# Layer 2's w_in decoded one stage sooner, its w_out sooner too, one output group of eight, and longer transfers in the plan for the first tiles

## The chip, the cores and the metric

The kernel runs on one core of one Trainium2 chip. The metric is the device time of one execution in microseconds (us), the median of several runs.

## The reference

What is computed is an attention in chunks, whose result goes through two layers of the same shape with different gates (cut to what matters):

```python
# attention, for each chunk of 32 queries (4 batches, 8 heads, 768 positions, 64 wide)
k_full = np.concatenate([mem_k, k[c0 - 16:c0 + 40]], axis=2)   # 8 memory rows, then the window
v_full = np.concatenate([mem_v, v[c0 - 16:c0 + 40]], axis=2)
out[c0:c0 + 32] = softmax(q_c @ k_full.T / sqrt(64)) @ v_full

x = out.transpose(0, 2, 1, 3).reshape(3072, 512)
# layer 1: w_in 512 x 2048, w_out 2048 x 512
h = x @ w_in;  x = (h * clip(h + 3, 0, 6) / 6) @ w_out
# layer 2: other weights
h = x @ w_in;  g = h if h >= 1, 0 if h <= -1, else ((h + 1) / 2) ** 2
out = g @ w_out
```

## The kernel before

Everything is fp32 on the outside; each product of two fp32 matrices is made of three matmuls on operands that are split into a high and a low part ("hi" and "lo"). The weights arrive as 64-bit words ("wpk"). A weight tile of 128x512 is turned into hi and lo on the chip, by `decoded` and what calls it: a load into `raw` (L318), a shift on ACT (L325) or on DVE (L327), a rebase on ACT (L331), a join on DVE (L335), a cast to hi on ACT (L303) and a subtraction for lo on DVE (L366).

Tokens come in six tiles of 512. Tiles 0 and 1 go through layer 1 directly, right behind their attention: `hidden` (matmuls L866 to L868, gate L875 on ACT and L878 on DVE, split into ghi L886 on ACT and glo L887 on DVE) and `project` (L902 to L904). Attention of a block is: scores (PE L748, from `q_sb` and the windows `kx` that POOL copies at L625 and L626), exponent (ACT L772), norm (DVE L778 to L782), a flip of the weights by TensorE (L789) whose result `tp` is copied to `tr` (L303, on ACT or DVE), the values (PE L800 into `pv`), and the split into xhi (ACT L847) and xlo (DVE L848). Before the first hidden matmuls stand nine matmuls on the identity (L1440) that only keep TensorE busy.

All later tiles go in pairs, by a scheme that needs seven products where the plain one needs eight. Layer 1 has the stages (0,1) and (0,2), layer 2 the stages (1,0), (1,1) and (1,2). A stage has eight steps of `hidden_pair` (PE L1027 to L1029; ACT copies a bank at L1010, DVE adds the other at L1014; gate: ACT L1074, DVE L1082) and output products. In stage (0,1) the output is `project`; in the others it is `out_pair` (PE L1264 to L1266), over groups of hidden steps. A group sums its products in PSUM, and where a stage has more than one group, the partial results are added up in `csum` (DVE L1242 and L1236, ACT L1234). `SEVEN` lists the groups of each stage: (0,2) has two groups of four, (1,0) and (1,1) one group of eight.

Layer 2's weights are decoded while layer 1 runs. `weight_pair` takes two w_in tiles: the decoding, four subtractions of 128x256 on DVE (L457), casts on ACT (L468, L471, L472) and subtractions on DVE (L469, L473, L476); its results go out to memory (`wfs`) and come back when they are used. For w_out it is `weight` and `combine_out` (subtractions L496, cast L509, subtraction L510, stores to `wcs`).

What sets the order of the work is a planner that is part of the kernel: every operation is added with an engine and a cost, a key (a due time in the planner's own units) and a list of tasks that must be done before; the planner runs a list schedule with a limited number of buffers (pools "w", "s", "in", "lv" and others), and the order that comes out is the order of the instructions on each engine. For a transfer the size that the planner reckons with is `kb`. It does not change the transfer itself.

The lines of the change: L617 in `load_block` (queries and keys of one block), L676 in `load_values` (values of one block), L1090 (`SEVEN`), L1406 (keys of `weight_pair`) and L1409 (keys of layer 2's w_out tiles).

Of the kernel before, what the change touches and what calls it, by code (L numbers as in the profile page):

```python
# [38 lines left out]
NK = 2 * NF  # L39
# [222 lines left out]
def fused_kernel(ctx: ExitStack, tc: tile.TileContext, qkv, qk, vv, wpk, const, out):  # L262
    nc = tc.nc
# [28 lines left out]
    add = plan.add  # L292
# [305 lines left out]
    def load_block(j, key):  # L598

        early = key < 0

        over = key > NF
        far = 3 * (not early)
        w = KB + KC if wide(j) else KB
        q = q_buf[j] = Buf(
            ["in"] + ["w"] * ((early or over) and not wide(j)), [128, NP * (QB + w)], F32, "q_sb",
            **({"w": 1} if early else {}),
        )  # L610
        if j < NEARLY:
            src = qkv[j, :, :WQ]
        else:
            src = qk[2 * (j - NEARLY):2 * (j - NEARLY) + 2].rearrange("g d w -> (g d) w")
        after = [*last_w, *later.get(j * NCH // NSB // 4, ())] if over else ()
        if not wide(j):
            add(("SP", 430), key - 6 - far * (key > 4) - 2.5 * early, lambda e: nc.sync.dma_start(tile_of(q), src), writes=[(q, 0)], kb=448, after=after, line="load")  # L617
            kx = kx_buf[j] = Buf(["w", "st"], [128, NP, 2, KC], F32, "kx", w=2, st=1)

            def windows(e):  # L620
                k = tile_of(q)[:, NP * QB:].rearrange("p (a t) -> p a t", a=NP)
                at = k[:, :, NMEM + CHUNK:KC + CHUNK]
                p, a, t = at.ap
                X = {"DVE": V, "POOL": G}[e]
                X.tensor_copy(tile_of(kx)[:, :, :, NMEM:], type(at)(at.tensor, at.offset, [p, a, (CHUNK, 2), t]))  # L625
                X.tensor_copy(tile_of(kx)[:, :, :, :NMEM], k[:, :, :NMEM].unsqueeze(2).to_broadcast([128, NP, 2, NMEM]))  # L626

            kx.made = add(("DVE", 700) if j < 2 else ("POOL", 1300), key - 5 - 3.5 * early, windows, [(q, 0)], [(kx, 0)])
            return
        k4 = lambda: tile_of(q)[:, NP * QB:].rearrange("p (a t) -> p a t", a=NP)  # L630
        add(
            ("SP", 430), key - 6 - far, lambda e: nc.sync.dma_start(
                k4()[:, :, :KB], src[:, NP * QB:].rearrange("p (a t) -> p a t", a=NP)
            ), writes=[(q, 1)], kb=256, after=after, line="load",
        )
        add(
            ("SP", 430), key - 6 - far, lambda e: nc.sync.dma_start(tile_of(q)[:, :NP * QB], src[:, :NP * QB]),
            writes=[(q, 0)], kb=192, after=after, line="load",
        )

        def spread(e):
            k = k4()
            cast(e, k[:, :, KB + NMEM:], k[:, :, NMEM + CHUNK:KC + CHUNK])
            cast(
                e, k[:, :, 2 * CHUNK:2 * CHUNK + 2 * KC].rearrange("p a (b t) -> p a b t", b=2)[:, :, :, :NMEM],
                k[:, :, :NMEM].unsqueeze(2).to_broadcast([128, NP, 2, NMEM]),
            )

        add([("DVE", 425), ("ACT", 560)], key - 4.5, spread, [], [(q, 1)])

    def load_values(s, key):


        early = key < 0
        late = s * SB >= 2 * T
# [4 lines left out]
        n = 0  # L660

        def load(x, c, m, row, rows, step, j):

            nonlocal n
            if j < NEARLY:
                src = qkv[j, row:row + rows, WQ + W * x:WQ + W * (x + 1)]
            else:
                src = vv[2 * (j - NEARLY) + x, row:row + rows, :]
            lines, rest = src.ap
            src = type(src)(src.tensor, src.offset, [lines, (lines[0] * step, m), rest])  # L670
            p = 64 * x + row % CHUNK
            queue = "ACT" if s == 0 and x else "SP"
            add(
                (queue, 400), min(key - 2, -7.2) if early else key - 8,
                lambda e: (nc.scalar if e == "ACT" else nc.sync).dma_start(tile_of(v)[p:p + rows, c:c + m], src),
                writes=[(v, n)], kb=1.7 * rows * m if early else rows * m, line="load v" + queue,  # L676
                after=[kx_buf[s].made] if queue == "ACT" else later.get(s // 4, ()),
            )
            n += 1
# [3 lines left out]
        while c < NSB:  # L683
            j, i = divmod(s * NSB + c, NCH)
# [8 lines left out]
        if not late:  # L693
# [3 lines left out]
            while c < NSB:  # L697
                m = 1
# [365 lines left out]
    def gate(l, p, t, f, key, h, psum=False):  # L1064
# [22 lines left out]

    raw_g = {}
    SEVEN = {
        (0, 2): ((0, 1, 2, 3), (4, 5, 6, 7)), (1, 0): (tuple(range(8)),), (1, 1): (tuple(range(8)),), (1, 2): (tuple(range(6)), (6, 7)),  # L1090
    }
    BASE = (0, 29.25, 57.25, 85.25, 113.25)
    GMOST = 20
# [270 lines left out]
    for n, (l, p) in enumerate(pairs):  # L1364
# [38 lines left out]
            pair_x(*pairs[n + 1], base + 25, [done[n, 7 if seven else 5]], ["w"] if seven else ["in", "lv", "w"])  # L1403
        if n == 0:
            for i in range(NF // 2):
                weight_pair(i, base + 22 + 4 * i, [done[0, 5]])  # L1406
        if n == 1:
            for i in range(NF // 2):
                raws = [weight(1, 2 * i + x, 1, base + 20 + step * (i + 0.5 * x) - 3, [done[1, 3]]) for x in range(2)]  # L1409
                combine_out(i, raws, base + 20 + step * (i + 0.5) + 1)  # L1410

    with tc.manual_schedule():
# [98 lines left out]
```

## Time and profile before

| | |
|---|---|
| time, median of 3 runs | 1062.2 us (1061.84, 1062.2, 1065.2) |
| the profiled execution | 1067.35 us |
| its span in the profile | 1065.3 us |
| TensorE (PE) busy in the span | 1036.6 us, 97% |
| VectorE (DVE) busy | 835.9 us, 78% |
| ScalarE (ACT) busy | 679.8 us, 64% |
| DMA | 289.18 MB, mean 271 GB/s |

The profile is that of one execution. Busy time of TensorE is that of its matmuls, which overlap: each 128x512 matmul is shown with some 0.39 us, while the next one starts about 0.23 us behind it. So a busy share says less than the count of matmuls in a stretch and the idle times that the timeline shows in square brackets, with what ended them. PEclk is the granted clock as a share of full speed.

### The profile page before, as it was taken

To read this page: it belongs to the slowest core of one execution; us is meant where nothing else is said; L and a number is where in the kernel's file an instruction comes from. 1 tells how busy PE (TensorE), PEld (TensorE's weight loads), DVE (VectorE), ACT (ScalarE), POOL (GpSimd) and SP (SyncE) were. 2 spreads that over 40 slices of the span, in tenths; PEclk is the share of its full clock that TensorE was granted. 3 is DMA by queue.
4 is the path that set the end of the run, shared out by engine and by line. 5 is a ranking of instruction groups with operands and counts; after the bars stand their busy time and mean duration, and the time that the engine had idled before them with its cause. 6 is when DMAs were issued, how large, how long until landed. Compare 5 with 4: busy or idle time off the path is not lost.

```text
span 1065.3 us, 19872 instructions
## 1 busy us (share of the span) xinstructions
PE 1036.6 (97%) x7381; PEld 842.6 (79%) x7381; DVE 835.9 (78%) x1439; ACT 679.8 (64%) x1427; POOL 27.2 (3%) x49
## 2 busy tenths in 40 slices
PE   6899999999999999999999999999999999999998
PEld 5677787788878887878778788888888888888886
DVE  4897489856876689789899997799765899658654
ACT  5897457634655586666785698655577655676461
POOL 4220000000000000000000000000000000000000
PEclk9999999999999999999999999999999999999999
DMA  8999878873988689999899799855774755965603
GB/s 244 345 358 359 332 237 273 285 243 112 321 282 258 198 300 368 417 399 390 309 404 399 282 344 391 311 178 188 228 266 151 282 169 177 334 223 198 191 34 79
DMA packets 153760, 289.18 MB, mean 271 GB/s; under 512 B 12352, under 2 KB 97984, under 8 KB 153664
## 3 DMA queue, kind: packets, MB, share of 16 engines
q1 hardware_dynamic: 153232, 287.62, 76.9%
q8 instruction: 58, 0.95, 0.4%
q10 hardware_dynamic: 432, 0.30, 0.1%
q14 instruction: 38, 0.31, 0.1%
HBM read 206.08 MB, written 81.79 MB: 270 GB/s over the span
## 4 chain that ended last, share of the span: by engine, by line
PE 67%; DVE 16%; DMA 11%; ACT 3%; issue 2%; SPq 1%; POOL 0%; DVEq 0%; POOLq 0%; ACTq 0%
PE ph L1027 10%; PE ph L1028 9%; PE ph L1029 9%; PE po L1265 7%; PE po L1266 7%; PE po L1264 7%; DMA raw<-wpk 5%; DVE glo L887 4%; PE py L902 3%; PE py L904 3%; PE py L903 3%; DVE raw L335 2%; PE ph L866 2%; DVE g L1224 2%; PE ph L868 2%
## 5 line engine op out<-in xcount | busy, mean ns | idle before, releaser
L886 ACT CAST ghi<-g 128x512 fp32r<-128x512 f32 x234 | 145.0, 621 | 119.1 <-PE po L1266 78.8
L887 DVE TENSOR_TENSOR glo<-g,ghi 128x512 fp32r<-128x512 f32 x234 | 158.7, 686 | 37.5 <-ACT ghi L886 37.2
L1027 PE MATMUL ph<-xop,wf 128*128 128x512 f32 x448 | 175.2, 391 | 3.2 <-DVE s L1014 1.9
L1028 PE MATMUL ph<-xop,wf 128*128 128x512 f32 x448 | 174.5, 390 | 0.8 <-DVE xop L977 0.8
L1029 PE MATMUL ph<-xop,wf 128*128 128x512 f32 x448 | 174.4, 389 | 0.0
L1265 PE MATMUL po<-glo,ws 128*128 128x512 f32 x420 | 163.6, 390 | 0.4 <-DVE glo L887 0.4
L1266 PE MATMUL po<-ghi,ws 128*128 128x512 f32 x420 | 163.4, 389 | 0.0
L1264 PE MATMUL po<-ghi,ws 128*128 128x512 f32 x420 | 163.4, 389 | 0.0
L1074 ACT ACTIVATE r<-s,bias 128x512 f32<-128x512 f32 x120 | 86.6, 724 | 58.7 <-DVE s L1014 57.8
L1014 DVE TENSOR_TENSOR s<-s,ph 128x512 f32<-128x512 f32 x120 | 81.8, 685 | 43.4 <-PE ph L1029 36.5
L1027 PEld LDWEIGHTS ph<-xop,wf 128*128 128x128 f32 x448 | 84.1, 188 | 24.1 <-DVE s L1014 4.2
L902 PE MATMUL py<-ghi,w 128*128 128x512 f32 x256 | 102.5, 401 | 0.0
L1010 ACT COPY s<-ph 128x512 f32<-128x512 f32 x120 | 70.6, 588 | 47.7 <-PE ph L1029 43.8
L903 PE MATMUL py<-glo,w 128*128 128x512 f32 x256 | 100.2, 391 | 0.2 <-DVE glo L887 0.2
L904 PE MATMUL py<-ghi,w 128*128 128x512 f32 x256 | 99.9, 390 | 0.0
L1028 PEld LDWEIGHTS ph<-xop,wf 128*128 128x128 f32 x448 | 84.1, 188 | 18.0 <-DVE xop L977 1.2
L1029 PEld LDWEIGHTS ph<-xop,wf 128*128 128x128 f32 x448 | 84.1, 188 | 17.6
L1265 PEld LDWEIGHTS po<-glo,ws 128*128 128x128 f32 x420 | 78.8, 188 | 17.6 <-DVE glo L887 1.2
L1264 PEld LDWEIGHTS po<-ghi,ws 128*128 128x128 f32 x420 | 78.8, 188 | 16.5
L1266 PEld LDWEIGHTS po<-ghi,ws 128*128 128x128 f32 x420 | 78.9, 188 | 16.1
L1082 DVE SCALAR_TENSOR_TENSOR g<-r,s 128x512 f32<-128x512 f32 x104 | 71.5, 690 | 24.3 <-ACT r L1078 10.1
L1224 DVE TENSOR_TENSOR g<-g 128x512 f32<-128x512 f32 x120 | 81.1, 687 | 1.4
(132 smaller groups left out, 1775.1 us busy)
## 6 DMA issues: line engine op xcount, KB each, us to landing
raw<-wpk SPq DMA_DIRECT2D x64, 512.0 KB
ws<-wcs SPq DMA_DIRECT2D x60, 512.0 KB
wf<-wfs SPq DMA_DIRECT2D x48, 512.0 KB
ws<-wos SPq DMA_DIRECT2D x90, 256.0 KB
wf<-wfs SPq DMA_DIRECT2D x48, 384.0 KB
wos<-w SPq DMA_DIRECT2D x32, 512.0 KB
wcs<-wc SPq DMA_DIRECT2D x32, 512.0 KB
w<-wos SPq DMA_DIRECT2D x32, 512.0 KB
```

The lines of the kernel that those rows point to most:

```text
L886: add(("ACT", act(T)), key, lambda e: A.copy(tile_of(ghi), g()), [of], [(ghi, 0)], line="split")
L887: add(("DVE", dve(T)), key + 0.1, lambda e: V.tensor_tensor(out=tile_of(glo), in0=g(), in1=tile_of(ghi), op=ALU.subtract,), [of, (ghi, 0)] ...
L902: P.matmul(y, w2hi, gh, start=first, stop=False)
L903: P.matmul(y, w2hi, gl, start=False, stop=False)
L904: P.matmul(y, w2lo, gh, start=False, stop=last)
L1027: P.matmul(q, whi()[:, m], xh, start=first, stop=False, skip_group_check=True)
L1028: P.matmul(q, whi()[:, m], xl, start=False, stop=False, skip_group_check=True)
L1029: P.matmul(q, wlo()[:, m], xh, start=False, stop=c == 1, skip_group_check=True)
L1224: ("DVE", dve(T)), key, lambda e: V.tensor_tensor(out=o(), in0=i0(), in1=i1(), op=op),
L1264: P.matmul(q, wt[:, 0, m], xh, start=begin, stop=False, skip_group_check=True)
L1265: P.matmul(q, wt[:, 0, m], xl, start=False, stop=False, skip_group_check=True)
L1266: P.matmul(q, wt[:, 1, m], xh, start=False, stop=end, skip_group_check=True)
```

## The change

Four things change. The planner reckons with longer transfers: the first blocks' queries and keys count 605 instead of 448, and the values of all blocks of tiles 0 and 1 count 1.95 per row instead of 1.7 (for the first) or 1 (for the others). Stage (0,2) gets one output group of eight steps instead of two of four. Layer 2's w_in pairs get keys from the start of stage (0,1) on, six units apart, and may begin when that stage's first hidden step is done, instead of keys from 22 units into the stage, four apart, and behind its sixth step. Layer 2's w_out tiles get keys 6 units sooner, 3.2 units apart, and may begin behind the second hidden step of stage (0,2) instead of the fourth; the keys of `combine_out` stay.

```diff
-            add(("SP", 430), key - 6 - far * (key > 4) - 2.5 * early, lambda e: nc.sync.dma_start(tile_of(q), src), writes=[(q, 0)], kb=448, after=after, line="load")
+            add(("SP", 430), key - 6 - far * (key > 4) - 2.5 * early, lambda e: nc.sync.dma_start(tile_of(q), src), writes=[(q, 0)], kb=605 if early else 448, after=after, line="load")
...
-                writes=[(v, n)], kb=1.7 * rows * m if early else rows * m, line="load v" + queue,
+                writes=[(v, n)], kb=(1.95 - 0.95 * late) * rows * m, line="load v" + queue,
...
-        (0, 2): ((0, 1, 2, 3), (4, 5, 6, 7)), (1, 0): (tuple(range(8)),), (1, 1): (tuple(range(8)),), (1, 2): (tuple(range(6)), (6, 7)),
+        (0, 2): (tuple(range(8)),), (1, 0): (tuple(range(8)),), (1, 1): (tuple(range(8)),), (1, 2): (tuple(range(6)), (6, 7)),
...
-                weight_pair(i, base + 22 + 4 * i, [done[0, 5]])
+                weight_pair(i, NK + 6 + 6 * i, [done[0, 0]])
...
-                raws = [weight(1, 2 * i + x, 1, base + 20 + step * (i + 0.5 * x) - 3, [done[1, 3]]) for x in range(2)]
+                raws = [weight(1, 2 * i + x, 1, base + 14 + 3.2 * (i + 0.5 * x) - 3, [done[1, 1]]) for x in range(2)]
```

How the order moves is shown at three places. The first is the attention of tile 0 on TensorE, the last instructions before the identity matmuls; L789 are the flips, L800 the values:

```order
 L748 MATMUL sc<-q_sb 32x64 x8
-L800 MATMUL pv<-tr,v_sb 64x32 x32
-L789 MATMUL tp<-ident,st 128x128 x8
-L800 MATMUL pv<-tr,v_sb 64x32 x64
 L789 MATMUL tp<-ident,st 128x128 x4
 L800 MATMUL pv<-tr,v_sb 64x32 x32
+L789 MATMUL tp<-ident,st 128x128 x4
+L800 MATMUL pv<-tr,v_sb 64x32 x32
+L789 MATMUL tp<-ident,st 128x128 x4
+L800 MATMUL pv<-tr,v_sb 64x32 x64
 L1440 LDWEIGHTS ident
```

Flips and values now take turns one by one. Behind them stand eight identity matmuls instead of nine, and 36 hidden matmuls instead of 21 ahead of the next block's scores.

On DVE, before, this stood ahead of the last two of these values (L303 into `tr` is the copy of a flip, L848 the xlo of tile 0):

```order
L782 TENSOR_TENSOR st<-st,sm 128x512
L335 SCALAR_TENSOR_TENSOR raw<-raw 128x512
L848 TENSOR_TENSOR xlo<-pv,xhi 128x2x128 x2
L327 TENSOR_SCALAR raw<-raw 128x512
L366 TENSOR_TENSOR w<-raw,w 128x512
L303 COPY tr<-tp 128x512
```

And in the changed kernel, behind the last norm (L782):

```order
L782 TENSOR_TENSOR st<-st,sm 128x512
L848 TENSOR_TENSOR xlo<-pv,xhi 128x2x128 x2
L327 TENSOR_SCALAR raw<-raw 128x512
L335 SCALAR_TENSOR_TENSOR raw<-raw 128x512
L366 TENSOR_TENSOR w<-raw,w 128x512
L335 SCALAR_TENSOR_TENSOR raw<-raw 128x512
L848 TENSOR_TENSOR xlo<-pv,xhi 128x2x128 x2
L327 TENSOR_SCALAR raw<-raw 128x512
L848 TENSOR_TENSOR xlo<-pv,xhi 128x2x128 x2
```

The flip's copy left this place, and the last xlo stands behind the second shift (L327). At the same place on ACT, before (`w` and `raw` belong to the first weight tiles, `xhi` to tile 0):

```order
L772 ACTIVATE st,sm<-sc,sm 128x64 x4
L847 CAST xhi<-pv 128x2x128 x2
L772 ACTIVATE st,sm<-sc,sm 128x64 x4
L325 ACTIVATE raw<-raw 128x512
L331 ACTIVATE raw<-raw 128x512
L847 CAST xhi<-pv 128x2x128 x2
L325 ACTIVATE raw<-raw 128x512
L303 CAST w<-raw 128x512
```

And on ACT in the changed kernel:

```order
L772 ACTIVATE st,sm<-sc,sm 128x64 x8
L847 CAST xhi<-pv 128x2x128 x2
L303 COPY tr<-tp 128x512
L847 CAST xhi<-pv 128x2x128 x2
L303 COPY tr<-tp 128x512
L331 ACTIVATE raw<-raw 128x512
L325 ACTIVATE raw<-raw 128x512
L303 CAST w<-raw 128x512
```

Two copies of flipped weights moved from DVE to ACT and stand ahead of all decoding there.

The second place is ACT some 108 us into the run, where a rebase (L331) stands ahead of a gate (L875), before:

```order
L303 COPY q_sb<-q_sb 128x4x56
L303 COPY q_sb<-q_sb 128x4x2x8
L886 CAST ghi<-r 128x512
L331 ACTIVATE raw<-raw 128x512
L875 ACTIVATE r<-ph,bias 128x512
```

And the same tile's rebase in the changed kernel:

```order
L303 CAST w<-raw 128x512 x2
L875 ACTIVATE r<-ph,bias 128x512
L325 ACTIVATE raw<-raw 128x512
L331 ACTIVATE raw<-raw 128x512
L886 CAST ghi<-r 128x512
```

The rebase now stands behind the gate, and its load is issued four transfers sooner.

The third place is DVE in stage (0,2), before, around the last but one w_in pair (numbers behind the names are the buffers'):

```order
L469 TENSOR_TENSOR wp1_5816<-raw_5659,wp0_5794 128x1024
L1082 SCALAR_TENSOR_TENSOR g_5823<-r_5811,s_5737 128x512
L473 TENSOR_TENSOR wp3_5830<-raw_5667,wp2_5803 128x512
L476 TENSOR_TENSOR wp3_5830<-raw_5667,wp2_5803 128x256
L1014 TENSOR_TENSOR s_5750<-s_5750,ph_5714 128x512
```

And around the last w_in pair in the changed kernel, which lies in stage (0,1):

```order
L469 TENSOR_TENSOR wp1_5653<-raw_5524,wp0_5645 128x1024
L473 TENSOR_TENSOR wp3_5665<-raw_5537,wp2_5659 128x512
L476 TENSOR_TENSOR wp3_5665<-raw_5537,wp2_5659 128x256
L887 TENSOR_TENSOR glo_5684<-g_4503,ghi_5678 128x512
L887 TENSOR_TENSOR glo_5715<-g_4756,ghi_5710 128x512
L1014 TENSOR_TENSOR s_5638<-s_5638,ph_5704 128x512
```

All eight pairs now stand ahead of the hidden steps of (0,2). Over the whole program the additions L1242 fall from 20 to 6; L1236 rises from 3 to 4, and L1234 falls from 5 to 4.

## Rows read from the trace of the kernel before

**Rows 1.** The page's first part: busy us, share of the span, instructions.

```profile
PE 1036.6 (97%) x7381; PEld 842.6 (79%) x7381; DVE 835.9 (78%) x1439; ACT 679.8 (64%) x1427; POOL 27.2 (3%) x49
```

**Rows 2.** Stretches: length, busy of PE, PEld, DVE, ACT, POOL, PEclk, DMA share, GB/s.

```profile
50.00:75.00 25.00, 23.52 (x282) 18.48 (x282) 24.67 (x50) 24.16 (x57) 3.01 (x5) 1.00 1.03 383
250.00:300.00 50.00, 50.00 (x521) 39.95 (x520) 39.96 (x78) 29.09 (x89) 0.00 (x0) 1.00 0.78 266
400.00:450.00 50.00, 49.76 (x219) 40.53 (x218) 43.62 (x68) 33.46 (x53) 0.00 (x0) 1.00 1.00 391
400.00:650.00 250.00, 245.32 (x1070) 199.38 (x1069) 231.45 (x384) 181.26 (x298) 0.00 (x0) 1.00 0.97 369
...
700.00:750.00 50.00, 50.00 (x222) 41.44 (x221) 47.70 (x71) 27.60 (x43) 0.00 (x0) 1.00 0.52 179
```

**Rows 3.** TensorE's timeline at the start: start, us, instruction, idle before and releaser.

```profile
29.40 1.14 PE L800 MATMUL pv<-tr,v_sb 64*64 64x32 f32 x64 [3.64 <-DVE tr L303]
30.47 3.80 PE L1440 MATMUL ph<-ident 128*128 128x512 bf16 x9
...
34.34 0.40 PE L867 MATMUL ph<-xlo,w 128*128 128x512 f32 x1
...
40.59 0.28 PE L748 MATMUL sc<-kx,q_sb 64*32 64x64 f32 x6 [1.25 <-POOL kx L626]
```

**Rows 4.** DVE's timeline ahead of the first hidden matmul.

```profile
27.72 0.43 DVE L327 TENSOR_SCALAR raw<-raw 128x512 uint32<-128x512 uint32 x1
...
33.44 0.74 DVE L848 TENSOR_TENSOR xlo<-pv,xhi 128x256 fp32r<-128x256 f32 x2
```

**Rows 5.** ACT's timeline ahead of the first hidden matmul.

```profile
30.54 0.71 ACT L325 ACTIVATE raw<-raw 128x512 uint32<-128x512 uint8 x1 [0.91 <-DMA raw<-wpk]
...
32.78 0.65 ACT L847 CAST xhi<-pv 128x256 fp32r<-128x256 f32 x2
```

**Rows 6.** Timeline at 108 to 116 us, ACT's row and TensorE's.

```profile
108.74 0.71 ACT L331 ACTIVATE raw<-raw 128x512 f32<-128x512 f32 x1 [4.97 <-DMA raw<-wpk]
...
110.83 0.50 PE L866 MATMUL ph<-xhi,w 128*128 128x512 f32 x1 [1.18 <-DVE r L878]
```

**Rows 7.** TensorE's waits from 400 to 650 us: releaser: us, times, longest.

```profile
PE ph L1027 <- DVE s L1014: 1.9, 4, 0.7
PE ph L1027 <- ACT s L1010: 1.3, 1, 1.3
PE ph L1028 <- DVE xop L977: 0.8, 1, 0.8
PE po L1265 <- DVE glo L887: 0.4, 1, 0.4
PE py L903 <- DVE glo L887: 0.2, 1, 0.2
```

**Rows 8.** Stretches of 2 us around the identity matmuls, same columns.

```profile
31.00:33.00 2.00, 2.00 (x6) 0.69 (x5) 1.40 (x3) 2.00 (x5) 0.72 (x1) 0.50 1.02 305
33.00:35.00 2.00, 2.00 (x8) 1.29 (x7) 2.00 (x5) 1.87 (x5) 1.90 (x3) 0.75 1.01 397
```

**Rows 9.** L469 over the whole run: durations in ns, first and last start.

```profile
L469 DVE TENSOR_TENSOR wp<-raw,wp x8: 1214/1220/1226, 383.5 to 466.3; 128x1024 fp32r<-128x1024 f32 x8
```

**Rows 10.** Timeline of DVE and TensorE around one of these waits.

```profile
455.07 1.21 DVE L469 TENSOR_TENSOR wp<-raw,wp 128x1024 fp32r<-128x1024 f32 x1
...
456.81 0.68 DVE L473 TENSOR_TENSOR wp<-raw,wp 128x512 fp32r<-128x512 f32 x1
...
457.41 0.42 DVE L476 TENSOR_TENSOR wp<-raw,wp 128x256 fp32r<-128x256 f32 x1
...
458.48 0.50 PE L1027 MATMUL ph<-xop,wf 128*128 128x512 f32 x1 [0.72 <-DVE s L1014]
```

**Rows 11.** DVE's groups from 360 to 620 us: count, busy us, mean ns, idle.

```profile
L335 DVE SCALAR_TENSOR_TENSOR raw<-raw 128x512 uint32<-128x512 uint32 x28 | 19.0, 688 | 0.8 <-ACT raw L331 0.7
...
L1242 DVE SCALAR_TENSOR_TENSOR csum<-po,csum 128x512 f32<-128x512 f32 x20 | 13.3, 684 | 0.0
```

## Prediction

> **What bounds the kernel now.** I read the page's first part, then TensorE's timeline for its gaps, then the engines that end each gap, then counts by stretch. TensorE is busy for 97% of the span, DVE for 78%, ACT for 64% [rows 1]. So nothing is to be had but the idle time of TensorE and stretches where its matmuls come slower than they can. In a fed stretch, from 700 to 750 us, 222 matmuls fit in 50 us [rows 2], that is 50 / 222 = 0.225 us each. By this measure I look for what is missing. The matmuls of the algorithm are the same in both kernels (the change reorders, and drops one identity matmul), so every gain must come from idle time, and there are three places.
>
> The first is the start. The values of tile 0's last block wait 3.64 us for a flip's copy by DVE, and the identity matmuls follow for 3.80 us [rows 3]. The first hidden matmul that needs xlo starts at 34.34 [rows 3], as DVE's xlo ends (33.44 + 0.74 = 34.18) [rows 4]; that xlo waits for its xhi, from 32.78 on ACT, which stood behind a shift that waited for the fourth weight tile until 30.54 [rows 5]. After some 5 us of hidden matmuls TensorE waits again, 1.25 us for POOL's copy of `kx`, until 40.59 [rows 3].
>
> The second is the middle of the direct stage: ACT stood 4.97 us on one weight tile, with a gate behind it, and TensorE waited 1.18 us for the gate's other half [rows 6].
>
> The third is stage (0,2), with its borders. From 400 to 650 us the waits of TensorE add up to 1.9 + 1.3 + 0.8 + 0.4 + 0.2 = 4.6 us [rows 7]. The count says more: 1070 matmuls, where five fed stretches would hold 5 x 222 = 1110; 40 x 0.225 = 9.0 us [rows 2]. Some of those 40 may be records that the trace lacks, so the loss lies between 4.6 and 9.0. The matmul after a wait starts slowly (0.50 for 0.39 us), and I take 6.0, nearer to the waits, since they have rows of their own.
>
> **The start.** With longer transfers in the plan, flips and values alternate, and two of the copies stand on ACT ahead of the decoding. So the 3.64 us shrink: the copy that ended them stood on DVE behind a join and a subtraction of weight tiles, and no longer does. What is late next is the fourth weight tile. It lands at 30.5 [rows 5], and on DVE its shift (0.43) now stands ahead of the last xlo (0.74) [rows 4]: some 30.5 + 0.43 + 0.74 = 31.7 for xlo's end, against 34.18 before. Hidden matmuls thus run 2.5 us sooner. They can't push the next scores forward, since these wait for `kx` until 40.6 as before [rows 3] (loads of queries keep their place on SP); but 36 hidden matmuls instead of 21 stand ahead of these scores, so that 15 x 0.225 = 3.4 us of work fill the time. From 31.7 to 40.6 there are 8.9 us, and 36 need 8.1 at the full rate.
>
> They do not get the full rate. From 31 to 33 us the granted clock is 0.50, from 33 to 35 it is 0.75 [rows 8], and before that TensorE had stood idle for 3.64 us. Identity matmuls take this time now; in the changed kernel hidden matmuls may stand in it. The nine identity matmuls show the price at half the clock, 3.80 / 9 = 0.42 us [rows 3]. Eight hidden ones at it take 3.4 us, about as long as the clock is low now (30.5 to some 34), so that 36 need 3.4 + 28 x 0.225 = 9.7, to 41.4, 0.8 us late; with 0.1 for a restart this leaves 3.4 - 0.9 = 2.5 us, which I take. Bounds: 3.4, with the clock back in time, and 0.5, if the fourth tile's cast is as late as it was and only the shift on DVE is saved.
>
> A page bears on this: the Trainium skill, "TensorE: Matmul & The Clock Gate", section "Part 1: The HAM clock gate", says that the array is at half its clock by default and after idleness, and that only sustained work brings it back. By that rule, work that is moved up to right behind an idle stretch runs at half rate, and the gain would be up to 1.7 us less than the 3.4 (half of the 3.4 us at half rate above); the trace agrees, with 0.50 behind the 3.64 us of idleness. It speaks against this part of the change, and would leave 1.7 instead of 2.5.
>
> **The middle.** The rebase that waited 4.97 us now stands behind the gate, and its load is issued four transfers sooner. TensorE's 1.18 us behind it would go, and half of that I count: -0.6. Bounds: -1.2 (all of it) and 0 (the ACT queue stands before another tile instead).
>
> **Stage (0,2).** Two things leave it. The eight w_in pairs, from 383.5 to 466.3 us now [rows 9], go ahead of it; one of their runs on DVE, 1.21 + 0.68 + 0.42 = 2.31 us, stood ahead of an addition for which TensorE waited 0.72 us [rows 10]. And one group of eight leaves out 14 additions into csum: 14 x 0.684 = 9.6 us of DVE [rows 11]; the additions that begin a csum come to one more, 0.7, and ACT has one less. None of this is on the path by itself: DVE has room in most stretches. What counts is that the hidden products' waits end on DVE's and ACT's adds and copies. Those are 1.9 + 1.3 = 3.2 of the 4.6 us, 70%; of the 6.0 us that is 4.2, which I take as the gain. The other 1.8 us (xop, glo) stay, since nothing there changes. Stages with one group of eight, as at 700 us, show what I expect: 222 matmuls at DVE's 47.70 of 50 [rows 2]. Bounds: -9.0 (all of it) and 0, if w_out's decoding, which is moved sooner by up to 35 us in the same stage, stands where w_in's stood.
>
> **What it puts elsewhere.** All eight pairs now lie in stage (0,1), spread over it, where about half of them lay before, at its end. A pair costs DVE two joins (2 x 0.688 [rows 11]), four 256-wide subtractions (4 x 0.42) and 2.31 us [rows 10], 5.4 us together. From 250 to 300 us DVE is busy 39.96 of 50 us [rows 2], so that it has 10 us to spare for one or two pairs; and of the 50 us from 400, in which half of the eight stand [rows 9], TensorE loses 0.24 (49.76 busy) [rows 2]. I put +0.7, one wait as in rows 10. Bounds: 0 and +5.
>
> **Sum.** -2.5 - 0.6 - 4.2 + 0.7 = -6.6 us. The profiled execution took 1067.35, 5.15 more than the median of 1062.2; from it this is 1060.75, and against the median **1055.6 us**.
>
> **Rivals.** (a) *The lead at the start does not come.* First hidden matmuls wait for the fourth tile's cast, at half clock: 0.5 instead of 2.5 us. For it: the wait of 0.91 us for that tile [rows 5]. Then -4.6, 1057.6. Still faster.
>
> (b) *The lead is swallowed.* From 50 to 75 us DVE is busy 24.67 and ACT 24.16 of 25 us, at a DMA share of 1.03 [rows 2]: TensorE runs at 23.52 behind them there, and a lead that it brings would end at the next gate. And in (0,2) the 1.3 us wait for ACT's copy [rows 7] stays under w_out's decoding. Nothing then comes of start and middle, and 2 us of (0,2): 1060.2, no change that can be told. Against it: ACT's decoding waits, for 0.91 us as early as 30 us [rows 5] and 4.97 at 104 [rows 6], so the engines aren't the bound all along.
>
> (c) *Slower: the pairs stop stage (0,1).* A pair in one run on DVE is 5.4 us. In rows 10 a run of 2.31 us cost 0.72, so the buffers of TensorE's products cover about 1.6 us; the rest is a loss. Eight pairs at 5.4 - 1.6 = 3.8 would be 30 us, were they all in one run ahead of the stage's own steps. It decides from (6.6 + 0.7 + 3.2) / 8 = 1.3 us a pair; at 1.5 the sum is -6.6 - 0.7 + 12 = +4.7, 1066.9. For it: the pairs' order on DVE is fixed, and what stands behind waits. Against it: the 0.24 us above, in which most of the same pairs stood beside projections of just this stage.
>
> **How the numbers follow.** About 0.3%, 3.2 us, is what a measurement of this kernel can tell from no change: faster is below 1059.0, slower above 1065.4. Chances: the forecast 0.46, (a) 0.16, (b) 0.25, (c) 0.13. So faster 0.62, within 0.3% 0.25, slower 0.13. The range goes from 1051.0, where start and middle give their most (-4.6) and (0,2) gives 7.3, between its 6.0 and 9.0, with the 0.7 left, to 1063.0, beyond (b); (c) and some of the rest are left out.
>
> **What would show it.** Right: tile 0's last values wait under 1 us, the first hidden matmul with xlo starts by 32, and from 400 to 650 us some 1090 matmuls stand, with no wait of L1027 above 0.5 us. Wrong at the start: hidden matmuls from 33.5 on. Wrong in (0,2): waits of L1027 for L1014 or L1010 as before, with L496 or L510 of w_out ahead of them on DVE. Case (c): between 230 and 430 us waits for L1014, L887 or L878 behind L457 or L469, a microsecond or more each. Case (b): an earlier first matmul, but the same time for the matmul that stands at 75 us.

## The result, and the profile after

The changed kernel took 1072.18 us (median of 6 runs, 1069.05 to 1073.49), the kernel before 1063.63 (6 runs, 1060.82 to 1065.59): a ratio of 1.0079, 95% interval 1.0056 to 1.0102. It is 8.4 us slower by this ratio (the medians lie 8.6 apart), where 6.6 us less were forecast, and outside the range.

The page's first part of the changed kernel, beside [rows 1]:

```profile
span 1071.2 us, 19872 instructions
...
PE 1040.4 (97%) x7380; PEld 842.0 (79%) x7380; DVE 826.5 (77%) x1422; ACT 680.8 (64%) x1430; POOL 26.9 (3%) x49
```

DVE has 9.4 us less to do, as the 14 additions fewer said it would, and the time is longer all the same. The start came sooner, though in this execution by less than forecast. TensorE's timeline of the changed kernel, beside [rows 3] (start, us, instruction, idle before and releaser):

```profile
28.01 1.72 PE L800 MATMUL pv<-tr,v_sb 64*64 64x32 f32 x55 [3.24 <-issue]
29.66 3.20 PE L1440 MATMUL ph<-ident 128*128 128x512 bf16 x8
...
32.93 0.44 PE L867 MATMUL ph<-xlo,w 128*128 128x512 f32 x1
```

The hidden matmul that needs xlo starts at 32.93 instead of 34.34, and 1.4 us sooner is not all: 36 of them, not 21, now stand before the next scores. The loss stands in stage (0,1). Three windows of the changed kernel, then the first two of them of the kernel before (columns as in [rows 2]); 290 to 320 lies in the middle of the stage:

```profile
225.00:400.00 175.00, 169.23 (x1692) 134.60 (x1690) 135.40 (x252) 111.42 (x287) 0.00 (x0) 1.00 0.85 290
290.00:320.00 30.00, 26.88 (x296) 20.63 (x295) 24.41 (x51) 22.04 (x64) 0.00 (x0) 1.00 1.00 359
400.00:650.00 250.00, 247.00 (x1072) 199.79 (x1072) 211.79 (x344) 169.03 (x279) 0.00 (x0) 1.00 0.92 339
```

```profile
225.00:400.00 175.00, 175.00 (x1727) 141.15 (x1726) 127.02 (x228) 104.53 (x277) 0.00 (x0) 1.00 0.74 245
290.00:320.00 30.00, 30.00 (x373) 23.97 (x372) 22.41 (x43) 18.20 (x59) 0.00 (x0) 1.00 0.87 283
```

Before, TensorE had no idle time at all from 225 to 400 us; now it has 5.8 us of it. DVE is busy 135 of 175 us, so it isn't full. What is full is the DMA, in the last pair of columns: the share of its engines rose from 0.74 to 0.85, and to 1.00 from 290 to 320 us. Who waits for what there is told by the waits of the changed kernel from 225 to 410 us (who waits, what it waits for: us in total, times, longest), TensorE's two longest first, then those of ACT and DVE that ended with a load of queries, of w_in or of a raw tile, the longest:

```profile
PE ph L1027 <- DVE g L1082: 2.7, 3, 1.0
PE tp L789 <- ACT xt L303: 1.4, 1, 1.4
...
ACT q_sb L303 <- DMA q_sb<-qk: 5.9, 2, 3.3
DVE q L420 <- DMA w<-wis: 5.0, 4, 2.0
...
DVE q_sb L303 <- DMA q_sb<-qk: 3.0, 3, 2.0
ACT raw L325 <- DMA raw<-wpk: 2.2, 2, 1.7
```

The two longest of these in the kernel before:

```profile
ACT q_sb L303 <- DMA q_sb<-qk: 3.6, 2, 2.3
DVE q L420 <- DMA w<-wis: 2.9, 3, 2.1
```

TensorE waits for DVE and ACT, and these stand before loads: queries (`qk`), layer 1's w_in (`wis`), raw weights. Such waits are not new. The same four groups come to 16.1 us in the change and to 7.5 before, where none of it reached TensorE; what is new is their length and that TensorE feels them. Two such chains, from the timelines of the changed kernel (ACT and TensorE at 297 us, DVE and TensorE at 339 us):

```profile
296.80 0.65 ACT L303 COPY q_sb<-q_sb 128x224 f32<-128x224 f32 x2 [3.29 <-DMA q_sb<-qk]
297.36 0.36 ACT L303 COPY xt<-pv 128x256 f32<-128x256 f32 x1
...
297.78 0.66 PE L789 MATMUL tp<-ident,st 128*128 128x128 f32 x4 [1.43 <-ACT xt L303]
...
338.81 0.69 DVE L420 TENSOR_TENSOR q<-w 128x512 f32<-128x512 f32 x1 [1.41 <-DMA w<-wis]
339.41 0.68 DVE L1082 SCALAR_TENSOR_TENSOR g<-r,ph 128x512 f32<-128x512 f32 x1
...
340.15 0.50 PE L1027 MATMUL ph<-xop,w 128*128 128x512 f32 x1 [1.04 <-DVE g L1082]
```

The copy of queries holds up ACT's row for 3.29 us; behind it stands a copy that TensorE needs for its next flips. At 338 us DVE stands 1.41 us before a weight tile, with a gate behind it.

Two more waits of that stage, 0.96 us at 300.79 and 0.72 us at 319.70, end on a gate that stands behind work of a w_in pair on DVE itself:

```profile
299.71 0.42 DVE L457 TENSOR_TENSOR raw<-raw 128x256 f32<-128x256 f32 x1
300.05 0.68 DVE L1082 SCALAR_TENSOR_TENSOR g<-r,ph 128x512 f32<-128x512 f32 x1
300.79 0.51 PE L1027 MATMUL ph<-xop,w 128*128 128x512 f32 x1 [0.96 <-DVE g L1082]
...
317.42 0.43 DVE L476 TENSOR_TENSOR wp<-raw,wp 128x256 fp32r<-128x256 f32 x1 [0.83 <-DMA wfs<-wp]
```

At 300 us the pair's work (a join L335, then L457) runs late, behind the stand of ACT at 297 us; at 317 us it stood 0.83 us until a store of an earlier result had landed. So late transfers and the pairs' own time on DVE meet there.

### The profile page after: what moved, and what is told of

Same layout as the page of the kernel before. It is cut to its first block, busy times and chain, and to the rows that moved or that the text cites. A ratio compares the mean times of both kernels' runs of the same rounds, so it can differ in the third digit from the quotient of the medians.

```text
span 1071.2 us, 19872 instructions
## 1 busy us (share of the span) xinstructions
PE 1040.4 (97%) x7380; PEld 842.0 (79%) x7380; DVE 826.5 (77%) x1422; ACT 680.8 (64%) x1430; POOL 26.9 (3%) x49
## 4 chain that ended last, share of the span: by engine, by line
PE 65%; DMA 15%; DVE 12%; ACT 4%; issue 1%; SPq 1%; POOL 0%; ACTq 0%; DVEq 0%; POOLq 0%
PE ph L1027 10%; PE ph L1028 9%; PE ph L1029 9%; PE po L1265 7%; PE po L1266 7%; PE po L1264 7%; DMA raw<-wpk 5%; PE py L902 3%; PE py L903 3%; PE py L904 3%; DVE glo L887 3%; DMA q_sb<-qk 2%; DMA w<-wis 2%; DVE g L1224 1%; ACT st L772 1%
## 5 line engine op out<-in xcount | busy, mean ns | idle before, releaser
L1027 PE MATMUL ph<-xop,wf 128*128 128x512 f32 x448 | 175.2, 391 | 0.9 <-DVE s L1014 0.9
L1265 PE MATMUL po<-glo,ws 128*128 128x512 f32 x420 | 164.2, 391 | 1.2 <-DVE glo L887 0.9
L1264 PE MATMUL po<-ghi,ws 128*128 128x512 f32 x420 | 163.7, 390 | 0.3 <-ACT ghi L886 0.3
L1014 DVE TENSOR_TENSOR s<-s,ph 128x512 f32<-128x512 f32 x120 | 81.9, 683 | 49.8 <-PE ph L1029 47.3
L1027 PEld LDWEIGHTS ph<-xop,wf 128*128 128x128 f32 x448 | 84.1, 188 | 21.3 <-DVE s L1014 2.5
L1010 ACT COPY s<-ph 128x512 f32<-128x512 f32 x120 | 70.4, 586 | 44.4 <-PE ph L1029 41.3
L1265 PEld LDWEIGHTS po<-glo,ws 128*128 128x128 f32 x420 | 78.8, 188 | 20.1 <-DVE glo L887 3.7
L1264 PEld LDWEIGHTS po<-ghi,ws 128*128 128x128 f32 x420 | 78.8, 188 | 17.6 <-ACT ghi L886 0.8
```

Source lines behind the costliest of these rows:

```text
L1027: P.matmul(q, whi()[:, m], xh, start=first, stop=False, skip_group_check=True)
L1264: P.matmul(q, wt[:, 0, m], xh, start=begin, stop=False, skip_group_check=True)
L1265: P.matmul(q, wt[:, 0, m], xl, start=False, stop=False, skip_group_check=True)
```

## The experiments

The kernels are compared with the kernel before by their times, and by where they gain and lose. For the second, the two profiles are lined up by TensorE's own work (matmul by matmul, in the order of each program), and the table gives how much later (+) or sooner (-) a kernel is than the profiled execution of before when the same work is done: at the points where before is at 238 us (stage (0,1) has begun), at 413 us (that stage is nearly over) and at 682 us (all of (0,2) is over), from where on nothing moves. Times in us; the ratio's interval is the 95% one.

| kernel | ratio of times (interval) | at 238 | at 413 | at 682 |
|---|---|---|---|---|
| the change, all four parts | 1.0079 (1.0056 to 1.0102) | -1.5 | +6.7 | +5.7 |
| e1: all but w_in | 1.0026 (1.0005 to 1.0048) | -7.2 | -7.8 | -2.0 |
| e2: w_in alone | 1.0058 (1.0041 to 1.0076) | -2.8 | +5.9 | +5.0 |
| e3: longer transfers alone | 0.9967 (0.9946 to 0.9987) | -6.6 | -6.0 | -7.5 |
| e4: group of eight alone | 1.0027 (1.0006 to 1.0049) | -3.3 | -2.8 | -1.3 |
| e5: the change, few stores | 0.9983 (0.9962 to 1.0004) | -10.1 | -10.6 | -8.3 |
| e6: the change, L469 three times | 1.0105 (1.0074 to 1.0136) | -6.8 | +7.8 | +9.3 |
| e7: w_out alone | 1.0059 (1.0039 to 1.0079) | -0.6 | -0.5 | +5.3 |
| e8: transfers, w_in a little sooner | 0.9983 (0.9960 to 1.0006) | -6.8 | -2.0 | -4.6 |
| e9: longer queries alone | 0.9994 (0.9980 to 1.0009) | -2.6 | -3.3 | -3.1 |
| e10: longer values alone | 0.9959 (0.9943 to 0.9975) | -5.0 | -4.7 | -6.6 |
| e11: e1 with few stores | 0.9973 (0.9955 to 0.9991) | -6.5 | -7.5 | -7.6 |
| e12: transfers longer still | 1.0023 (1.0006 to 1.0040) | -2.9 | -1.8 | -2.9 |

One caution on the column "at 238". Up to there before, e2, e4 and e7 hold the same instructions in the same order, and are at 0, -2.8, -3.3 and -0.6; the change, e1, e3, e5, e6, e8 and e11 share another order, and are at -1.5, -7.2, -6.6, -10.1, -6.8, -6.8 and -6.5. So one profiled execution says up to 3.3 and 8.6 us more or less than another of the same code about the first 238 us. Nor is a profiled execution the median of its kernel: that of before lies 3.7 us above the median of the six runs, those of e1, e4, e5 and e12 lie 2.9 to 4.2 below theirs, so the last column alone does not rank the kernels. What a part does there is read from the means of the two groups (-1.7 and -6.5) and from the timed runs; the columns behind it are read by their differences, which repeat better: (0,1) with the moved pairs costs 8.2 (the change) and 8.7 (e2).

**Which part.** First the change without the w_in part:

```diff
-                weight_pair(i, NK + 6 + 6 * i, [done[0, 0]])
+                weight_pair(i, base + 22 + 4 * i, [done[0, 5]])
```

> The changed kernel with the w_in pairs' old keys (22 units into stage (0,1), four apart); the other three parts stay. Theory 1, the w_in pairs' place costs the time: the changed kernel lost 8.3 us against before in its profile between 300 and 410 us, where the moved pairs stand; this goes, and the time is 1063 to 1065, no more than 2 us off the kernel before, with TensorE's waits in that stretch under 1.5 us. Rival 2, the new plan of the first tiles costs it (the lead of 4.4 us is lost between 165 and 220 us and stage (0,1) comes out of step): the time stays at 1070 or above. Rival 3, the group of eight or w_out's earlier keys cost it: 1070 or above too, with the loss behind 437 us.

Measured: +0.26%, 2.8 us. From 238 to 413 us it loses nothing (-7.2 to -7.8): the whole loss of (0,1) belongs to w_in's place. But 2.8 us stay, and they stand in (0,2), from -7.8 to -2.0; rival 3 has a part in it. Then that line alone, in the kernel before:

> The kernel before with the w_in pairs' new keys alone. Theory 1: the same waits in stage (0,1) as in the changed kernel, about +8 us, 1070 to 1073, less what (0,2) gains without the pairs (some 2 us). Rival 2 and rival 3: within 2 us of before, or faster by the 2 to 3 us of waits that the pairs cause in (0,2).

Measured: +0.58%, 6.2 us. Stage (0,1) costs 8.7 us, and (0,2) gives 0.9 back (+5.9 to +5.0).

> The kernel before with the longer transfers in the plan alone (both lines). Theory 1: a lead of some 4 us up to 165 us, of which 1 to 1.5 are left at 225 us, and nothing lost in (0,1): 1062, -1.5 us. Rival 2: the lead is lost and (0,1) loses 5 us or more: 1068 or above.

Measured: -0.33%, 3.5 us faster, with lines 617 and 676 alone. Rival 2 is out: the new plan of the first tiles' transfers is the part that pays.

> The kernel before with one output group of eight in stage (0,2) alone. Theory 1: 14 additions fewer on DVE, a part of the 4.6 us of waits from 400 to 650 us goes: -1 to -3 us, 1061 to 1063, and nothing changes ahead of 400 us. Rival 3: slower by 2 us or more, with waits for glo (L887) ahead of L1265 in the output group.

Measured, with line 1090 alone: +0.27%, 2.9 us, where a gain was expected; in its profile (0,2) costs 1.5 us. The waits of TensorE from 400 to 650 us in this kernel:

```profile
PE ph L1027 <- ACT s L1010: 2.0, 1, 2.0
PE ph L1027 <- DVE s L1014: 1.9, 4, 0.7
PE po L1265 <- DVE glo L887: 1.1, 2, 0.7
...
```

The waits for L1014 are the same four, 1.9 us, as in [rows 7], with 14 additions fewer on DVE, and those for glo grew from 0.4 (L1265) to 1.1. The additions were not what TensorE waited for.

**What it is about the place.** Two kernels keep the changed kernel's order on every engine. One stores less:

```diff
-    wfs = dram.tile([NF // 2, 4, 128, 1024], F32, name="wfs")
+    wfs = dram.tile([NF // 2, 4, 128, 256], F32, name="wfs")
...
-                    wfs[i, x, :, :m], flat(tile_of(b)).bitcast(F32)),
+                    wfs[i, x], flat(tile_of(b))[:, :256].bitcast(F32)),
...
-            src = [(wfs[i, x, :, :256 * shapes[x][0]], ("wfs", i, x)) for x in range(4)]
+            src = [(wts[i, x % 2, :, :256 * shapes[x][0]], ("wfs", i, x)) for x in range(4)]
```

> The changed kernel, every instruction in the same order on every engine, but layer 2's w_in stores write 256 of 768 or 1024 columns (their loads read layer 1's tiles, as many bytes as before), so the output is not the reference's: 4.2 MB stored instead of 14.7. Theory A, the pairs in stage (0,1) cost TensorE through their transfers (loads of queries and of layer 1's weights land later, and ACT and DVE stand before them): of the 8.3 us that stage (0,1) lost against before, 4 or more go, 1064 to 1068. Theory B, they cost it through DVE's and ACT's time in a row: nothing changes, 1071 to 1073, with the waits at 297, 300, 319 and 340 us as they were.

Measured: 0.9983, which is 1.8 us under before and 10 us under the change. Stage (0,1) loses nothing (-10.1 to -10.6). Its window from 225 to 400 us, and all that ACT and DVE wait for loads of queries, of w_in and of raw tiles from 225 to 410 us:

```profile
225.00:400.00 175.00, 175.00 (x1725) 140.60 (x1724) 144.56 (x268) 121.24 (x303) 0.00 (x0) 1.00 0.81 271
```

```profile
ACT raw L325 <- DMA raw<-wpk: 0.2, 1, 0.2
```

TensorE is fed for 175.00 of 175 us with DVE busier than in the change (144.56, since all stands 9 to 17 us sooner). Of the 5.9 + 5.0 + 3.0 + 2.2 us that the change's rows stood before these loads 0.2 are left. (Waits for tiles that were stored shortly before and come back stay, as in before: ACT's and DVE's for `ymid` and `xmid` are 4.6 us here, 8.2 before.) What moved is megabytes: in these 175 us, by the DMA part of the page (packets, MB, GB/s) of before, of the change, of e5:

```profile
DMA packets 25123, 42.93 MB, mean 245 GB/s; under 512 B 2049, under 2 KB 17153, under 8 KB 25103
```

```profile
DMA packets 27216, 50.76 MB, mean 290 GB/s; under 512 B 2309, under 2 KB 17106, under 8 KB 27195
```

```profile
DMA packets 28831, 47.43 MB, mean 271 GB/s; under 512 B 2455, under 2 KB 20247, under 8 KB 28809
```

The change brings 7.8 MB more through the stretch, and the engines are at 1.00 where the waits are. How the stored bytes hold up the loads this kernel does not tell apart. One way is the transfers themselves: the queries that ACT waits for at 297 us are issued from 287.2 on and copied at 296.80, 9.6 us later; in e5 it is at most 6.6 us (278.5 to 285.1), and ACT does not wait. The other is the queue that issues them, SP: from 280 to 300 us it stood 3.9 us in the change until stores to `wfs` had landed, and not at all for them in the same work of e5 (272 to 292 us), so later loads also start later. Both come with the stored bytes.

The other kernel adds DVE's time and no transfer:

```diff
-        add(("DVE", dve(1024)), key - 0.1, lambda e: V.tensor_tensor(
-            out=two(bs[1]), in0=whole(), in1=two(bs[0]), op=ALU.subtract), [lo, hi, (bs[0], 0)], [(bs[1], 0)])
+        add(("DVE", dve(1024)), key - 0.1, lambda e: [V.tensor_tensor(
+            out=two(bs[1]), in0=whole(), in1=two(bs[0]), op=ALU.subtract) for _ in range(3)], [lo, hi, (bs[0], 0)], [(bs[1], 0)])
```

> The changed kernel in its own order, but the wide subtraction of each w_in pair (L469, 1.22 us) is done three times into the same tile: 2.44 us more of DVE in each of eight pairs, 19.5 us in all, no transfer more. Theory A: DVE is busy 135 of 175 us there and waits for transfers, so it takes up most: +0 to +3 us. Theory B: each pair's run on DVE grows by 45%, and the loss in the stage by as much or more: +5 to +15 us, 1077 or above.

Measured: +1.05% (4 runs), 2.8 us more than the change for 19.5 us of DVE, as theory A expected, though the two intervals overlap; in its single profile the stage costs 14.6 instead of 8.2 us, more than the timed runs say. So DVE's time isn't free where its row already waits for loads, but by either number two thirds or more of the 19.5 us cost nothing. And the pairs' DVE work by itself is not enough for the loss: without the stores the same work costs the stage nothing.

> The kernel before with w_out's earlier keys alone. From the runs so far (all four parts +8.4, transfers alone -3.5, group alone +2.9, w_in alone +6.2, all but w_in +2.8 us) the sum leaves +2.8 to +3.4 us for it: 1066 to 1067 where before has 1063.6, with new waits in stage (0,2), where w_in and w_out are then decoded side by side. If the parts don't add up and w_out alone costs nothing: 1063 to 1064.

Measured, with line 1409 alone: +0.59%, 6.3 us, twice what the sum left for it, all of it in (0,2) (-0.5 to +5.3), in small pieces. The parts don't add up: -3.5 + 2.9 + 6.2 + 6.3 = 11.9, and all four together cost 8.4. Moving w_in out of (0,2) makes room for w_out there: the change as a whole gains 1.0 us in (0,2), while without the w_in part it loses 5.8 (e1).

The same trial on that second loss, the kernel of e1 with the three edits of e5:

> As the run with the w_in pairs back at their old place (+2.8 us), with w_in's stores cut to 256 columns as in the run with few stores (4.2 instead of 14.7 MB; the output is not the reference's). In stage (0,2) that run lost 5.8 us against before, with w_in and w_out decoded side by side and the DMA engines 96% busy. Theory A, there too the loss comes by transfers: 4 us or more of it go, 1061 to 1063. Theory B, it comes from DVE and ACT, whose work is the same: +1 to +3 us, as it was.

Measured: 0.9973 against e1's 1.0026; 5.6 us go, and in its profile the whole 5.8 us of (0,2) (-7.5 to -7.6). TensorE's waits from 400 to 650 us, first of e1, then of e11:

```profile
PE ph L1027 <- DMA wf<-wis: 2.9, 2, 2.3
PE ph L1027 <- DVE s L1014: 1.8, 5, 0.9
PE po L1265 <- DVE glo L887: 0.8, 1, 0.8
PE po L1264 <- ACT ghi L886: 0.7, 1, 0.7
...
```

```profile
PE po L1265 <- DVE glo L887: 0.8, 1, 0.8
PE ph L1027 <- DVE s L1014: 0.6, 2, 0.4
PE ph L1027 <- DMA wf<-wis: 0.5, 1, 0.5
```

In e1 TensorE waits for a load of hidden weights itself. And the waits for L1014, which look like DVE's, fall from 1.8 to 0.6 us when nothing but stored bytes is taken away. This holds where w_in and w_out are decoded side by side. In the change, whose pairs have left (0,2), fewer stores bring nothing there: e5 loses 2.3 us in that stage (-10.6 to -8.3), where the change gains 1.0.

**Something better.** The longer transfers with the pairs moved a little, and then the two lines apart:

```diff
-                weight_pair(i, base + 22 + 4 * i, [done[0, 5]])
+                weight_pair(i, base + 18 + 4.5 * i, [done[0, 4]])
```

> The longer transfers in the plan, and the w_in pairs only a little sooner than before: from 18 units into stage (0,1), 4.5 apart, behind its fifth step. Theory A: they then stand in the end of (0,1), where the last tiles' queries are through, and cost nothing there: as with the transfers alone, 0.3% under before, or another 0.1 to 0.2% less where a pair leaves (0,2). Theory B: each pair that moves costs about 1 us: at or above before.

Measured: 0.9983, not better than the transfers alone (0.9967); the two intervals overlap. In its profile the end of (0,1) costs 4.8 us and (0,2) gives 2.6 back. From 380 to 410 us:

```profile
DVE raw L327 <- DMA raw<-wpk: 3.4, 1, 3.4
ACT raw L331 <- DMA raw<-wpk: 3.1, 1, 3.1
...
PE py L902 <- DVE ysb L934: 2.1, 1, 2.1
```

DVE's row stands 3.4 us before a raw tile, and TensorE then waits for what is behind it, in this profile with half the granted clock for a few matmuls after.

> The kernel before with the longer transfer of the first blocks' queries and keys alone (605 instead of 448). The two lines together gave -3.5 us. If the gain is the turn of flips and values on TensorE and the flips' copies on ACT, whichever line brings that order brings -2.5 to -3.5; the other 0 to -1. By the order of the instructions this line changes the rows from the first scores on; I expect the larger part here: -2 us, 0.998.

Measured, with line 617 of the change alone: 0.9994, no difference. This line alone doesn't bring the turn of flips and values of the change: the last values still wait, for 3.62 us, now for a copy on ACT, and the first hidden matmul with xlo starts at 34.57.

> The kernel before with the longer transfers of the values of tiles 0 and 1 alone (1.95 instead of 1.7 and 1). Changes the order only behind the second block's flips. -1 us, 0.999; if the gain sits here alone, -3.5.

Measured, with line 676 alone: 0.9959 (0.9943 to 0.9975), 4.4 us faster than before. The smaller part was expected here; it is the whole of the gain, and this kernel beats both the kernel before and the change. Yet it has not the order that the gain was put down to: flips and values of tile 0 stand as in before. Its timeline there:

```profile
27.46 0.42 PE L800 MATMUL pv<-tr,v_sb 64*64 64x32 f32 x9 [2.11 <-DVE tr L303]
28.48 1.72 PE L800 MATMUL pv<-tr,v_sb 64*64 64x32 f32 x55 [0.60 <-issue]
...
34.64 0.40 PE L867 MATMUL ph<-xlo,w 128*128 128x512 f32 x1
```

The first hidden matmul with xlo is no sooner than before (34.34). What this kernel shares with the change is that more hidden matmuls, 30 (36 in the change, 21 before), stand ahead of the next scores, and that the wait of 1.25 us for `kx` [rows 3] is gone. No run has that alone, so which of the moved instructions pays stays open. It is before with one edit:

```diff
-                writes=[(v, n)], kb=1.7 * rows * m if early else rows * m, line="load v" + queue,
+                writes=[(v, n)], kb=(1.95 - 0.95 * late) * rows * m, line="load v" + queue,
```

The last kernel goes further on both lines (cut to the changed terms, those of the change on the left):

```diff
-605 if early else 448
+800 if early else 448
...
-(1.95 - 0.95 * late) * rows * m
+(2.4 - 1.4 * late) * rows * m
```

> Transfers in the plan longer again (800 for queries and keys, 2.4 for values), nothing else. If a later landing in the plan only has to be late enough to bring flips and values to take turns: as with 605 and 1.95, -2 to -4 us. If the plan now idles for data that is there: 0 to +3 us.

Measured: 1.0023 (1.0006 to 1.0040). More is not better: this plan is slower than before by 2.4 us in the timed runs, though its one profile, the fastest of its 12 runs, is 2.9 us sooner. Flips and values don't take turns in it either (eight flips together, then four), and the last values wait 1.53 us.

## Why the prediction was wrong

**The start (-2.5) and the middle (-0.6): right in size, the way to it in part.** In the change's own profile the signs did not come: the last values still wait 3.24 us, and the first hidden matmul with xlo starts at 32.93, where "by 32" was said. In the six other profiles with this order (e1, e3, e5, e6, e8, e11) they did: that wait is gone, and the matmul starts between 29.86 and 31.53, against 33.90 to 34.59 in the four profiles with the order of before. Where before is at 45 us, the seven are 2.8 us sooner in the mean and e2, e4 and e7 are level with it (0.1 sooner), so the start gave some 2.7. In times the part alone brings -3.5 us (e3), where -3.1 stood. That the sum fits is partly luck, though: e10 has as much without the flips and values taking turns and without an earlier xlo, so what the term of 2.5 was built on is one way to the gain and not a condition of it.

The half clock came, but not for hidden matmuls. In the changed kernel's profile the rows from 25 to 28 and 30 to 32 us:

```profile
25.00:28.00 3.00, 0.00 (x0) 0.00 (x0) 1.11 (x2) 1.03 (x2) 0.03 (x1) 0.58 1.05 340
30.00:32.00 2.00, 2.00 (x6) 0.76 (x5) 0.84 (x3) 2.00 (x5) 0.00 (x0) 0.50 1.07 235
```

And of e3, the same order without the idle time, one such row and TensorE's timeline:

```profile
30.00:32.00 2.00, 1.61 (x6) 0.80 (x5) 1.44 (x4) 1.11 (x2) 0.00 (x0) 1.00 1.11 242
...
26.97 3.60 PE L1440 MATMUL ph<-ident 128*128 128x512 bf16 x8
...
31.39 0.50 PE L867 MATMUL ph<-xlo,w 128*128 128x512 f32 x1 [0.39 <-DVE xlo L848]
```

In the change's profile the idle 3.24 us before the last values are still there ("issue", while DVE and ACT were busy for a third of them), and the granted clock is 0.50 (1.2 GHz) behind them. The 1.00 in e3's row is not to be trusted: the first entry of the clock in that trace begins at 31.34 us, and before it the eight identity matmuls start 0.42 us apart, the price at half the clock in the prediction, though TensorE was busy all of 25 to 28 us. So the half rate there does not hang on that idle time. The Trainium skill ("TensorE: Matmul & The Clock Gate", Part 1) has half the clock by default as well as after idleness; the trace agrees with both. What the prediction had wrong is whom it hits: it let eight hidden matmuls run at half rate, and in e3 the identity matmuls take nearly all of it again, the hidden ones following 0.23 us apart from 31.72 on. What made the 3.24 us in one execution and not in another stays open.

The middle's waits [rows 6] were in part that one execution: e2, with the same instructions there, passed the stretch from 99 to 123 us 2.7 us quicker, and e2, e4 and e7 gain 1.7 there in the mean; the seven with the change's order gain 2.1, which leaves 0.4 of the 0.6 for the change. The profiled execution stood 5.15 us above the median, and the prediction took its waits as the code's.

**Rival (b), the lead swallowed, does not hold.** Its sign, the same time for the matmul at 75 us, did not come: there the change's profile is 2.9 us sooner than before and e3's 4.0. The change's profile does lose some 3 us of its lead between 150 and 238 us, with the clock at 0.50 from 200 to 203 us, but e1, e3 and e11 keep theirs through the same instructions.

**What it puts elsewhere (+0.7, bounds 0 to +5): the step that failed.** It measured +8.2 and +8.7. The sum counted what a pair costs DVE, and read DVE's spare time in [rows 2]. The last two columns of the same rows were not counted: a DMA share of 0.78 from 250 to 300 us, and a pair brings two raw loads and four stores, 2.9 MB (2 x 0.52 + 1.84), into it. With the pairs the share is 1.00 from 290 to 380 us, where it was 0.79, and without most of the stored bytes (e5) the stage costs -0.5 us instead of 8.2. The evidence that was held against rival (c), half of the pairs beside projections at 0.24 us, came from a stretch where no queries of the attention are loaded any more (the last are issued at 357 us); the DMA share was 1.00 there too [rows 2], and it cost 0.24. So a full DMA alone does not make the loss. That it takes a late load ahead of work that TensorE needs soon fits both stretches, but no run tests it. Rival (c) had the right stage and sign (it put the turn at 1.3 us a pair; eight pairs at 8.2 us are 1.0 a pair, and the missing gain of (0,2) did the rest), and only part of the cause: the pairs' run on DVE does stand ahead of gates (at 300 and 317 us), but it costs nothing without the stores; what makes it cost is transfers that land late for engines that take their work in order.

**Stage (0,2) (-4.2): wrong as well.** It came to -1.0: 1072 matmuls stand from 400 to 650 us, where some 1090 were the sign and 1070 stood before. The waits that the term was made of did mostly go. The changed kernel's waits from 400 to 650 us, beside [rows 7]:

```profile
PE ph L1027 <- DVE s L1014: 0.9, 2, 0.5
PE po L1265 <- DVE glo L887: 0.9, 1, 0.9
...
PE po L1264 <- ACT ghi L886: 0.3, 1, 0.3
```

Those of L1027 for L1014 and L1010 fell from 3.2 to 0.9 us, and to 0.7 in e2, which moves the w_in pairs alone. The step that failed is that such a wait, once gone, is a gain of as many us: the output products now wait 1.2 us for halves of the gate (L1264 and L1265), where it was 0.4, and the rest goes in pieces too short for this table. In e2 the waits for xop (L977) grow from 0.8 to 1.5 instead. Nor do the waits follow the pairs alone: e5, whose pairs are gone from the stage as well, has 2.9 us of them, and e11, which keeps the pairs there, 0.6. The 14 additions brought nothing (e4); the prediction rightly held that they are not on the path. The bound of 0 named w_out's decoding in place of w_in's; with w_in still there it costs 5.8 us (e1, e7), and for e1 the stored bytes are what limits (e11). For the change's (0,2), without w_in, the one profile of e5 does not show that, and what limits there stays open.

The Trainium skill's page "DMA: Bandwidth & Descriptors", section "Bandwidth", names about 358 GB/s as what each of two cores gets when both stream from the memory that they share, and measures up to 425 GB/s for one core whose neighbour is idle. The trace moved 359 GB/s at a share of 1.00 (the change, 290 to 320 us), but 391 from 400 to 450 us [rows 2], between the two figures: for loads and stores together 358 is no ceiling here, and the measurement decides.

Open is why the group of eight alone costs 1.5 (its profile) to 2.9 us (its times). Its transfers are not more (0.97 as before); the 2.0 us wait for a copy on ACT at 602 us, at the start of the next stage, is in its profile, but no run took it apart.

## What to carry to other kernels

When a step moves, count its bytes in the stretch it moves into, beside the DMA share there, before its engine time. Here a stretch at 0.79 went to 1.00, and the price was paid by other transfers, whose readers stand in order ahead of the work that TensorE waits for; the same share cost next to nothing (0.24 us in 50) in a stretch without loads of queries. A wait for an engine that isn't full is followed one step further back, to what that engine itself waited for; a kernel that keeps the order and takes away only bytes tells whether the wait is the engine's own or that of its transfers. And where one execution lies 5 us above the median, a wait seen in it alone is no term of a sum. A sum that fits is no proof of its terms either: e10 has the gain of the start without the order that was to bring it.

## What the runs showed of the hardware

Two executions of the same instructions differed by up to 8.6 us over the first 238 us; the DMA engines' share from 0 to 225 us is 0.90 in the profile of before, 0.93 in e3's and 0.94 in e1's. The change and e2, which hold the same pairs in stage (0,1), agree there within half a us (8.2 and 8.7). Bytes stored for one part of the work held up loads of another by microseconds at a share of 0.85 in the mean over 175 us; it was 1.00 from 290 to 380 us. And 19.5 us of extra work on an engine that was waiting for loads cost 2.8 us by the timed runs (6.4 by one profile).
